# Holding GpSimd behind the first half of a Newton norm, in a fused cosine attention and MLP kernel

## Chip, cores and metric

One core of one Trainium2 chip. The metric is the device time of one execution in microseconds (us). A time is about 1.8 us longer than the span from the first to the last instruction that the same execution's profile gives.

## The reference, cut to what matters

```python
q_n = q / (np.linalg.norm(q, axis=-1, keepdims=True) + 1e-06)      # batch 8, 12 heads, 448 x 64
k_n = k / (np.linalg.norm(k, axis=-1, keepdims=True) + 1e-06)
scores = np.matmul(q_n, k_n.transpose(0, 1, 3, 2)) / tau
... softmax, @ v ...
h = x @ w_in                                  # 3584 x 768 @ 768 x 2048
g = h * (1.0 / (1.0 + np.exp(-1.702 * h)))
return (g @ w_out).astype(np.float32)
```

## The kernel before

A planner in Python simulates the engines, orders all operations and emits them in that order. GpSimd (POOL) scales q and k by their inverse norms, squares some of the q and casts v; VectorE (DVE) computes the norms. The planner takes the two to share a port of SBUF and treats it as one slot ("port") that a GpSimd operation or a norm takes. In the emitted program the slot is made real in one direction only: a GpSimd port user waits, by a semaphore wait that the planner adds (the "made wait" below), for the last VectorE port user before it in the order. "Heads" below are pairs of heads, numbered 0 to 47. Of the VectorE lines named later, L568 is the gate of the MLP's activation, and L497 and L445 normalise attention outputs.

```python
# Plan.emit
insts = emit()
insts = insts if isinstance(insts, tuple) else (insts,)
...
if ("port", 1) in takes:
    if eng == "DVE":
        port = insts[-1]
    elif port is not None:
        link(insts[0], port)          # a semaphore wait of GpSimd on VectorE
```

A norm of a group of one to three heads is planned in two operations, `norm_a` and `norm_b`. Each gives the port back at its end, so GpSimd operations may be planned between them.

```python
def norm_a(grp):
    ...
    nc.vector.tensor_scalar(out=y.bitcast(I32), in0=a.bitcast(I32), scalar1=-0.5, scalar2=RS_MAGIC, ...)   # L282
    nrms[grp] = a, y, t
    newton(grp, RS_A, RS_B)                    # returns nothing: port becomes None

def newton(grp, ca, cb):
    a, y, t = nrms[grp]
    nc.vector.scalar_tensor_tensor(out=t, in0=y, scalar=-ca, in1=y, ...)      # L295
    nc.vector.tensor_tensor(out=t, in0=t, in1=a, op=ALU.mult)                 # L298
    nc.vector.scalar_tensor_tensor(out=y, in0=t, scalar=cb, in1=y, ...)       # L299

def norm_b(grp):                               # a second newton, then 3 more
    ...
    last = nc.vector.tensor_tensor(out=y, in0=y, in1=t, op=ALU.mult)          # L310
    ...
    return last
```

## Time and profile before

| | before |
|---|---|
| median of the first 3 runs (lowest, highest) | 434.37 us (433.66, 434.76) |
| time of the profiled execution, its span | 436.03 us, 434.2 us |
| busy: TensorE, VectorE, ScalarE, GpSimd | 420.0, 242.1, 290.3, 175.1 us |
| TensorE's idle time in the span | 14.2 us |

TensorE (PE) is busy nearly throughout, so the lines to read are those of what it waited for; they are in the prediction.

### The profile page before, as it was taken

What the parts mean: (1) busy time and instruction counts of PE and PEld (TensorE: products, weight loads), DVE (VectorE), ACT (ScalarE), POOL (GpSimd) and SP (SyncE); (2) the same over time, 40 slices, a digit from 0 to 9 for tenths busy, and PEclk for the clock granted to TensorE, in tenths of its full rate; (3) what the DMA queues carried; (4) which work ended last, traced back from release to release, by engine and by line L of the source; (5) the groups of instructions that cost most, each with busy time, mean ns of one, the idle gap of its engine ahead of it and who ended that gap; (6) DMA issues with size and microseconds to landing.
All of it is one profiled execution on the core that took longest, in us unless ns stands there. A gap on an engine that the chain in (4) does not pass through costs nothing.

```text
span 434.2 us, 11090 instructions
## 1 busy us (share of the span) xinstructions
PE 420.0 (97%) x4438; PEld 260.7 (60%) x4438; DVE 242.1 (56%) x621; ACT 290.3 (67%) x460; POOL 175.1 (40%) x229
## 2 busy tenths in 40 slices
PE   7899999997999999999999999999999999999996
PEld 7668886653555555555556555565656556555564
DVE  5866887879885677838766555563332343123200
ACT  5989678955877778978794876767682864233321
POOL 0831995294868758373882817261100000000000
PEclk9999999999999999999999999999999999999999
DMA  8899997966999999787999576855112121211122
GB/s 215 201 206 272 240 195 223 261 127 169 182 223 190 197 244 223 171 183 176 170 190 220 125 175 143 167 107 111 49 26 70 31 61 43 56 38 36 38 72 74
DMA packets 98099, 64.03 MB, mean 147 GB/s; under 512 B 56320, under 2 KB 93056, under 8 KB 98048
## 3 DMA queue, kind: packets, MB, share of 16 engines
q1 hardware_dynamic: 92320, 57.03, 57.8%
q0 software_dynamic: 5696, 6.29, 8.8%
q8 instruction: 35, 0.57, 0.6%
q14 instruction: 16, 0.13, 0.1%
q10 hardware_dynamic: 32, 0.01, 0.0%
HBM read 45.61 MB, written 11.01 MB: 130 GB/s over the span
## 4 chain that ended last, share of the span: by engine, by line
PE 82%; DVE 7%; ACT 4%; issue 2%; POOL 2%; DMA 1%; SPq 0%; ACTq 0%; POOLq 0%
PE mm L611 34%; PE mm L534 15%; PE mm L552 11%; PE avp L431 8%; PE sp L405 7%; PE sp L467 2%; PE mm L484 2%; ACT et L416 2%; DVE n L269 2%; PE mm L581 2%; DVE gT L568 2%; DVE y L282 1%; DMA k<-in_k_dram 1%; ACT sq L263 1%; PE tps L375 1%
## 5 line engine op out<-in xcount | busy, mean ns | idle before, releaser
L416 ACT ACTIVATE et<-sp 112x896 f16<-112x896 f32 x192 | 170.0, 919 | 30.9 <-PE sp L405 25.2
L611 PE MATMUL mm<-w_out,gT 128*128 128x384 f16 (+1 forms) x912 | 158.4, 323 | 0.0
L611 PEld LDWEIGHTS <-gT 128*128 128x128 f16 x912 | 83.9, 98 | 60.6 <-issue 11.0
L568 DVE SCALAR_TENSOR_TENSOR gT<-th,mm 128x448 f16<-128x448 f16 x112 | 66.8, 615 | 64.2 <-ACT th L563 64.2
L563 ACT ACTIVATE th<-mm 128x448 f16<-128x448 f32 x128 | 67.6, 549 | 42.8 <-PE mm L534 36.3
L534 PE MATMUL mm<-xT,w_in 128*128 128x448 f16 x408 | 85.3, 353 | 3.2 <-DVE gT L568 3.0
L269 DVE TENSOR_REDUCE n<-sq 112x8 f32<-112x512 f32 x96 | 63.8, 679 | 22.2 <-ACT sq L263 12.9
L623 ACT ACTIVATE ost<-mm 128x384 f32<-128x384 f32 (+1 forms) x57 | 27.7, 487 | 62.2 <-PE mm L611 61.8
L534 PEld LDWEIGHTS <-w_in 128*128 128x128 f16 x408 | 37.7, 98 | 39.8 <-issue 8.9
L359 POOL CAST vt<-v 112x256 f16<-112x256 f32 x90 | 34.0, 402 | 58.6 <-PE avp L431 52.3
L552 PE MATMUL mm<-xT,w_in 64*128 64x448 f16 x528 | 57.1, 349 | 0.0
L343 POOL TENSOR_TENSOR qks<-k,y 112x512 f16<-112x512 f32 x38 | 39.6, 1042 | 34.6 <-DVE y L310 17.9
L431 PEld LDWEIGHTS <-et 112*128 112x128 f16 x1152 | 43.4, 97 | 14.7 <-issue 4.2
L431 PE MATMUL avp<-vt,et 112*128 112x65 f16 x1152 | 47.0, 193 | 0.5 <-DVE xf L445 0.4
L442 DVE RECIPROCAL rcx<-avp 128x4 f32<-128x4 f32 x72 | 12.9, 179 | 60.9 <-PE avp L431 60.9
L262 POOL TENSOR_TENSOR sq<-q 112x512 f32<-112x512 f32 x33 | 34.1, 1039 | 24.4 <-ACT et L416 9.0
L405 PE MATMUL sp<-qkT 64*128 64x448 f16 x288 | 43.3, 353 | 0.0
L343 POOL TENSOR_TENSOR qks<-q,y 112x512 f16<-112x512 f32 x38 | 39.6, 1042 | 0.0
L552 PEld LDWEIGHTS <-w_in 64*128 64x128 f16 x528 | 25.6, 94 | 20.9
L263 ACT ACTIVATE sq<-k 112x512 f32<-112x512 f32 x48 | 30.3, 635 | 3.0 <-DMA k<-in_k_dram 3.0
L445 DVE TENSOR_TENSOR xf<-avp,rcx 128x256 f16<-128x256 f32 x72 | 30.5, 424 | 2.5
L405 PEld LDWEIGHTS <-qkT 64*128 64x128 f16 x288 | 13.4, 94 | 14.6 <-issue 6.3
(48 smaller groups left out, 282.9 us busy)
## 6 DMA issues: line engine op xcount, KB each, us to landing
k<-in_k_dram SPq DMA_DIRECT2D x48, 224.0 KB, 4.6
q<-in_q_dram SPq DMA_DIRECT2D x48, 224.0 KB, 4.7
v<-in_v_dram SPq DMA_DIRECT2D x48, 224.0 KB, 4.2
w_in<-in_moe_w_in_dram POOLq DMA_DIRECT2D x2, 1536.0 KB, 15.5
w_out<-in_moe_w_out_dram POOLq DMA_DIRECT2D x2, 1536.0 KB, 15.7
out_dram<-ost SPq DMA_DIRECT2D x7, 336.0 KB, 4.7
out_dram<-ost SPq DMA_DIRECT2D x8, 288.0 KB, 3.2
out_dram<-ost SPq DMA_DIRECT2D x8, 240.0 KB, 3.1
```

Source lines behind the costliest of these rows:

```text
L262: return nc.gpsimd.tensor_tensor(out=sqs[x, ti], in0=src, in1=src, op=ALU.mult)
L263: return nc.scalar.activation(out=sqs[x, ti], in_=src, func=AF.Square)
L269: nc.vector.tensor_reduce(out=n2s[grp][:, x - grp[0], ti], in_=sqs.pop((x, ti)), axis=AX.X, op=ALU.add,)
L343: return eng.tensor_tensor(out=qkss[x][:, 1 - ti].rearrange("p c j d -> p j c d"), in0=src, in1=rss[x][:, ti, :, :, None].to_broadcast((P, ...
L405: nc.tensor.matmul(out=sp[:, j, :S], lhsT=keys(x, j, c), rhs=queries(x, j, 0, S), start=True, stop=True,)
L416: nc.scalar.activation(out=e[:, : 2 * S].rearrange("p (j s) -> p j s", j=2), in_=sps.pop(key)[:P, :, :S], func=AF.Exp, scale=inv_tau, **kw,)
L431: nc.tensor.matmul(out=ps[:, (D + 1) * t : (D + 1) * (t + 1)], lhsT=exps[x, c][:, q0 : q0 + 128], rhs=values(x, c, D * j, D * j + D + 1), ...
L534: nc.tensor.matmul(out=ps[:, :S], lhsT=w_in_sb[:, kk, 128 * m : 128 * (m + 1)], rhs=xTs[b, kk][:, :S], start=(kk == 0), stop=(kk == KT1 - 1),)
L552: insts.append(nc.tensor.matmul(out=mms[b, m + i][:, :S], lhsT=w_in_sb[rows, kk, 128 * (m + i) : 128 * (m + i + 1)], rhs=xTs[b, kk][rows, :S],
L563: nc.scalar.activation(out=ths[key], in_=mms[key][:, :S], func=AF.Tanh, scale=0.851)
L568: nc.vector.scalar_tensor_tensor(out=gT[:, m, (b % 2) * S : (b % 2 + 1) * S], in0=ths.pop((b, m)), scalar=1.0, in1=mms.pop((b, m))[:, :S], ...
L611: nc.tensor.matmul(out=mms[b2, t, n][:, : c1 - c0], lhsT=gT[:, kk, 128 * t : 128 * (t + 1)], rhs=w_out_sb[:, kk, c0:c1], start=(kk == 0), ...
```

## The change

Its intent: the first half of a norm shall hold back GpSimd's next port users by the same made wait that every other VectorE port user causes. `norm_a` now returns its last instruction (L299), so `port` holds it in place of `None`.

```diff
-        newton(grp, RS_A, RS_B)
+        return newton(grp, RS_A, RS_B)
 
     def newton(grp, ca, cb):
...
-        nc.vector.scalar_tensor_tensor(
+        return nc.vector.scalar_tensor_tensor(
             out=y, in0=t, scalar=cb, in1=y, op0=ALU.add, op1=ALU.mult
         )
```

Nothing else moves: the instructions of every engine stand in the same order in both programs.

## The prediction

> **What bounds the kernel now.** I read the page first: the busy shares, the row of TensorE in the forty slices, and the chain that ended last.
>
> ```profile
> PE 420.0 (97%) x4438; PEld 260.7 (60%) x4438; DVE 242.1 (56%) x621; ACT 290.3 (67%) x460; POOL 175.1 (40%) x229
> ...
> PE   7899999997999999999999999999999999999996
> ...
> PE 82%; DVE 7%; ACT 4%; issue 2%; POOL 2%; DMA 1%; SPq 0%; ACTq 0%; POOLq 0%
> ```
>
> TensorE is the bound almost everywhere, so only what removes an idle stretch of TensorE can shorten the span. The row shows two slices that are not full away from both ends' ramps: the tenth digit is a 7, that is 97.7 to 108.6 us (a slice is 434.2 / 40 = 10.86 us). Next I asked for TensorE's waits between 60 and 130 us (what it waited for, total us, times, longest):
>
> ```profile
> PE mm L534 <- DVE gT L568: 3.0, 2, 2.9
> PE mm L507 <- DVE xs L497: 0.9, 1, 0.9
> PE avp L431 <- DVE xf L445: 0.4, 2, 0.3
> ```
>
> All three point at VectorE, which is in order: something in its queue ahead of the gate (L568) and of the normalisation (L497) was late. The same view from 130 us to the end lists nothing, and TensorE is busy 50.00 of 50 us in each of the stretches 200 to 250, 300 to 350 and 350 to 400. The timeline from 96.5 to 103.2 us (start, duration) names the culprit:
>
> ```profile
> 96.51 0.74 POOL L359 CAST vt<-v 112x256 f16<-112x256 f32 x2
> ...
> 97.21 1.04 POOL L262 TENSOR_TENSOR sq<-q 112x512 f32<-112x512 f32 x1
> 97.26 4.11 DVE L282 TENSOR_SCALAR y<-n 112x48 int32<-112x48 int32 x1
> ...
> 98.20 2.13 POOL L359 CAST vt<-v 112x256 f16<-112x256 f32 x6
> ...
> 100.28 1.04 POOL L262 TENSOR_TENSOR sq<-q 112x512 f32<-112x512 f32 x1
> ...
> 102.01 1.14 DVE L568 SCALAR_TENSOR_TENSOR gT<-th,mm 128x448 f16<-128x448 f16 x2
> ...
> 102.68 0.73 PE L534 MATMUL mm<-xT,w_in 128*128 128x448 f16 x3 [2.86 <-DVE gT L568]
> ```
>
> L282, the first instruction of a norm, has a median of 189 ns over its 13 executions; here it takes 4110 and ends at 101.37, just after GpSimd's run of square, six casts and square ends at 101.32. The gates behind it come 4 us late, no PSUM bank is freed, and TensorE stands still for 2.86 us. The chain that ended last says the same in its steps at 97.34 (4.04 us of L282) and then 102.68 (TensorE).
>
> **What the Trainium skill says.** "SBUF — State Buffer", section "SBUF: two separate sides": the port pair that VectorE and GpSimd share is an exclusive lock held for the whole instruction, and the loser is blocked fully. The 4.11 us agree. "VectorE: DVE Perf Modes", section "The perf-mode tier table": a tensor_scalar from SBUF in a 4-byte type gets the 2x mode and tensor_tensor does not; with the section on the 2x_2P mode that makes L282 a user of both read ports. The trace agrees in that L282 is the one hit hardest. "Perfetto Trace Analysis", section "GPSIMD Engine Instruction": GpSimd's spans should be timed by their start-to-start spacing. Here that is 1.00 us for a square or scale (recorded 1.04), and I use it.
>
> **The change part by part.** It adds no arithmetic. The first half of a norm used to return nothing, and the planner stores what a VectorE port user returns as "the last port user"; with nothing stored, GpSimd operations planned after it got no wait at all until the second half was emitted. Now they wait for the first half's last instruction (L299). So it touches only GpSimd operations planned between the two halves of one norm. I walked the planner's order of the kernel before: 13 norms of this kind, of which 6 have such operations, 15 in all. In the other seven (those that begin with heads 12, 21, 27, 36, 39, 42 and 45) no GpSimd user lies between the halves and nothing changes. So the 0.82 of L282 at 128.61 stays: what it met was a scale planned before it. The six:
>
> - Heads 15 to 17 (97 us): square of 18, casts 15 to 17, square of 19. The square of 18 is held; the cast before it ends at 97.25, so L282 at 97.26 finds the port free. Four instructions at 0.19 + 0.21 + 0.21 + 0.21 and three gaps of 0.03 end the half at about 98.15 instead of 102.09: VectorE gains 3.9 us. TensorE's stalled matmul needs the first of the two gates, whose tanh is done at 97.28 + 0.54 = 97.82; the gate now ends near 98.7, before TensorE asks at 99.82. **TensorE gains 2.86 us**, all of the gap.
> - Heads 10 and 11 (66 us): scale of q 9 and cast 10. Its four instructions run from 65.89 to 68.28, 0.71 + 0.98 + 0.30 + 0.30. The first waits for an earlier scale that stays (to 66.6); the other three then take about 0.65, ending at 67.26 instead of 68.28. The normalisation (L497) moves from 68.83 to 67.8 and TensorE's 0.89 gap goes. But the scale of q 9, held from 66.52 to 67.35, ends at 68.4, and the transposes of head 9 would now start at 68.12 and need it half way: 0.2 is given back. **TensorE gains 0.7 us.**
> - Heads 18 to 20 (114 us): the half takes 0.70 + 0.33 + 0.31 + 0.97 and gaps = 2.4 us; alone 0.9. VectorE gains 1.5 us. TensorE's waits near it are 0.26 and 0.18 for L445, so **about 0.3 us**.
> - Heads 24, 30, 33: L282 ran in 0.19 in all three (143.65, 178.55, 201.57), no stall to win. The held operations are casts of values needed tens of us later and one square. **Zero.**
>
> GpSimd pays: the square of 18 moves from 97.21 to 98.25, the run ends at 102.35 instead of 101.32; the square of 21 moves by about 1.2, a cast pair by 0.5 to 3. GpSimd then idled anyway, 5.72 us before 107.04 and 3.17 before 122.34, both for the second half of the norm (L310), which VectorE now reaches about 3 us earlier. So its delay is hidden. VectorE's reduction of the square of 18 stands behind the second gate, whose tanh ends at 99.26; the square ends at 99.25. No new wait.
>
> Sum on TensorE: 2.86 + 0.7 + 0.3 = 3.9 us. What of it lasts? Its input is far ahead: head 15's transposes are issued at 109.11, land about 3.5 us later (the median), and its scores start at 123.11; later heads have more. TensorE's clock is full in every slice. I keep 0.8 of it, 3.2 us: 434.4 - 3.2 = **431.2 us**.
>
> **The rivals.**
> 1. The stall at 97.26 is a matter of 50 ns: had VectorE come that much earlier it would have had the port first. In runs without the profiler it may do so. For: 0.05 us between the two starts. Against: one norm later (114.42) loses as well, and the three runs agree within 1.1 us, while 3 us would show. If true, the gain is about 1 us: 433.4.
> 2. The made wait takes the place of the lock: GpSimd held for a late VectorE delays scales, transposes and reductions, and TensorE waits for these. For: VectorE is busy 4.90 of 5 us from 97 to 102, so holding on it is risky; casts wait in order behind the held square. Against: GpSimd idles right after each of these runs, and head 15 has 10 us to spare. If true: 434 to 436.
> 3. The gain is given back: DMA is at 9 tenths from 108 to 174 us, and TensorE 3 us earlier could meet a transfer or the activation engine. For: that row of DMA. Against: no TensorE wait on a DMA is in the list, and loads start when scales free their buffers, which come earlier too. If true, half remains: 432.5.
> 4. All of the 3.9 us lasts, and VectorE, further ahead, removes some of the other gaps of 0.15 to 0.2 us too: 430.2.
>
> **Range and chances.** The main theory (3.2 us) and rival 4 together 0.65, rival 3 0.15, rival 1 0.12, rival 2 0.08. The middle stays at 431.2; eight times in ten I expect 429.9 to 433.5. Two per cent would be 8.7 us, more than twice all the TensorE waits found, so faster by over 2% gets 0.02; slower by over 2% needs a new wait of 9 us, which nothing in the trace offers: 0.02; within 2%: 0.96.
>
> **What would show it right or wrong.** Right: L282 has no execution over 1 us; TensorE's 2.9 us wait for L568 near 100 us is gone; the tenth digit of its row is 9; VectorE's busy time falls by 5 to 7 us (4110 - 190 ns, 1.5 and 1.0 us, all from the first half); GpSimd's first square after the norm at 97 starts just after L299 ends. Wrong: TensorE shows a new wait on a GpSimd scale (L343) or a DMA transpose, or on L269's followers because reductions wait for held squares; or TensorE's idle time is as long as before with other names beside it. If the gap goes and the span stays, rival 3 holds.

## The result

| | before | after |
|---|---|---|
| median of 6 runs (lowest, highest) | 434.15 us (433.39, 435.02) | 431.94 us (431.67, 433.22) |
| ratio, 95% interval | | 0.9956 (0.9936 to 0.9976) |
| span of the profiled execution | 434.2 us | 430.0 us |
| TensorE busy, idle | 420.0, 14.2 us | 419.9, 10.1 us |
| VectorE busy | 242.1 us | 236.5 us |

A ratio is the mean time of one kernel's fast runs over that of the other's of the same rounds, so it is not quite the ratio of the medians. The interval excludes 1, though the gain is under 2%. The change is a gain of 2.2 us by the medians, inside the predicted range, but the two profiled spans differ by 4.2 us. That gap is the main question of the experiments.

The page of the kernel after (busy times, TensorE's row of forty slices, the chain that ended last):

```profile
PE 419.9 (98%) x4438; PEld 261.2 (61%) x4438; DVE 236.5 (55%) x621; ACT 290.5 (68%) x460; POOL 175.4 (41%) x229
...
PE   7889999999999999999999999999999999999996
...
PE 86%; ACT 4%; DVE 3%; issue 2%; POOL 2%; DMA 1%; SPq 0%; ACTq 0%; POOLq 0%
```

The tenth digit is 9 now, and VectorE's share of the chain fell from 7% to 3%. Of TensorE's three waits between 60 and 130 us one is left, of 0.2 us in place of 3.0:

```profile
PE mm L534 <- DVE gT L568: 0.2, 1, 0.2
```

The timeline of the kernel after at the stretch that was at 97 us (start, duration; the bracket is idle time before the instruction and what ended it):

```profile
96.03 0.75 POOL L359 CAST vt<-v 112x256 f16<-112x256 f32 x2
...
96.78 0.18 DVE L282 TENSOR_SCALAR y<-n 112x48 int32<-112x48 int32 x1
...
96.92 3.56 PE L534 MATMUL mm<-xT,w_in 128*128 128x448 f16 x18 [0.15 <-DVE gT L568]
...
97.48 0.21 DVE L299 SCALAR_TENSOR_TENSOR y<-t,y 112x48 f32<-112x48 f32 x1
97.61 0.61 DVE L568 SCALAR_TENSOR_TENSOR gT<-th,mm 128x448 f16<-128x448 f16 x1
97.83 1.04 POOL L262 TENSOR_TENSOR sq<-q 112x512 f32<-112x512 f32 x1 [1.04 <-issue]
```

L282 finds the port free and takes 0.18 us; the square is held for 1.04 us (the view names no releaser, "issue", but the wait on L299 is what the edit added) and starts 0.14 us after L299 ends at 97.69; TensorE runs 18 matmuls in one piece.

The other stretch with a visible TensorE gap, at 66 us, before:

```profile
66.52 1.04 POOL L343 TENSOR_TENSOR qks<-q,yv 112x512 f16<-112x512 f32 x1
66.64 0.98 DVE L295 SCALAR_TENSOR_TENSOR t<-y 112x32 f32<-112x32 f32 x1
...
68.89 0.27 PE L507 MATMUL mm<-ident,xs 112*128 112x112 f16 x2 [0.89 <-DVE xs L497]
69.00 0.56 PE L367 MATMUL tps<-ident,qks 112*128 112x112 f16 x8
```

and after:

```profile
66.91 0.19 DVE L295 SCALAR_TENSOR_TENSOR t<-y 112x32 f32<-112x32 f32 x1
...
67.63 1.04 POOL L343 TENSOR_TENSOR qks<-q,yv 112x512 f16<-112x512 f32 x1 [0.79 <-DVE y L299]
...
68.21 0.27 PE L507 MATMUL mm<-ident,xs 112*128 112x112 f16 x2
68.31 0.79 PE L367 MATMUL tps<-ident,qks 112*128 112x112 f16 x8
```

TensorE's gap of 0.89 is gone, and the transposes of head 9 take 0.79 in place of 0.56, because half of them wait for the scale that was held.

**A ruler that leaves the start out.** Executions differ by up to 1.9 us before 66 us, where nothing of the change acts yet. So I measure from the start of the first L282 (heads 10 and 11) to that of the sixth (heads 24 on), both from the timeline. Before:

```profile
65.89 0.71 DVE L282 TENSOR_SCALAR y<-n 112x32 int32<-112x32 int32 x1
...
143.65 0.19 DVE L282 TENSOR_SCALAR y<-n 112x48 int32<-112x48 int32 x1
```

and after:

```profile
66.17 0.71 DVE L282 TENSOR_SCALAR y<-n 112x32 int32<-112x32 int32 x1
...
139.39 0.19 DVE L282 TENSOR_SCALAR y<-n 112x48 int32<-112x48 int32 x1
```

That is 143.65 - 65.89 = 77.76 us before and 139.39 - 66.17 = 73.22 after. From the sixth to the end it is 434.2 - 143.65 = 290.55 and 430.0 - 139.39 = 290.61 us. The whole difference arises between 66 and 144 us, and nothing of it is given back later.

### The profile page after: what moved, and what is told of

It is laid out like the page before. It is cut to its first block, busy times and chain, and to the rows that moved or that the text cites. A ratio compares the mean times of both kernels' runs of the same rounds, so it can differ in the third digit from the quotient of the medians.

```text
span 430.0 us, 11091 instructions
## 1 busy us (share of the span) xinstructions
PE 419.9 (98%) x4438; PEld 261.2 (61%) x4438; DVE 236.5 (55%) x621; ACT 290.5 (68%) x460; POOL 175.4 (41%) x229
## 4 chain that ended last, share of the span: by engine, by line
PE 86%; ACT 4%; DVE 3%; issue 2%; POOL 2%; DMA 1%; SPq 0%; ACTq 0%; POOLq 0%
PE mm L611 34%; PE mm L534 17%; PE mm L552 11%; PE avp L431 8%; PE sp L405 7%; PE sp L467 2%; PE mm L484 2%; ACT et L416 2%; PE mm L581 2%; DMA k<-in_k_dram 1%; ACT sq L263 1%; DVE n L269 1%; POOL qks L343 1%; PE tps L375 1%; POOL n L326 1%
## 5 line engine op out<-in xcount | busy, mean ns | idle before, releaser
L445 DVE TENSOR_TENSOR xf<-avp,rcx 128x256 f16<-128x256 f32 x72 | 30.6, 425 | 2.5
```

## The experiments

The first four ran on one chip beside the same 11 runs of the kernel before.

### e1: the kernel before again (no edit)

> The kernel before, a second time against itself. The changed kernel's profiled span was 4.2 us shorter than that of before, but its median time only 2.2 us shorter. Theory A (the stall of L282 near 97 us, 4.1 us in the first trace, happens in every run): ratio 1.000 and a profiled span of about 434, L282 over 4 us again. Rival (a matter of 50 ns: VectorE sometimes comes first): the new trace has an L282 near 97 us well under 4 us or the run spans fall in two groups some 2 us apart.

Measured: 433.70 us, ratio to itself 1.0012 (0.997 to 1.0054), profiled span 431.5 at full clock. Its timeline:

```profile
97.32 1.04 POOL L262 TENSOR_TENSOR sq<-q 112x512 f32<-112x512 f32 x1
97.37 1.04 DVE L282 TENSOR_SCALAR y<-n 112x48 int32<-112x48 int32 x1
...
97.51 3.82 PE L534 MATMUL mm<-xT,w_in 128*128 128x448 f16 x18 [0.15 <-DVE gT L568]
98.31 2.13 POOL L359 CAST vt<-v 112x256 f16<-112x256 f32 x6
98.44 0.32 DVE L295 SCALAR_TENSOR_TENSOR t<-y 112x48 f32<-112x48 f32 x1
```

and its TensorE waits between 60 and 130 us:

```profile
PE mm L507 <- DVE xs L497: 0.9, 1, 0.9
PE avp L431 <- DVE xf L445: 0.5, 2, 0.3
PE mm L534 <- DVE gT L568: 0.2, 1, 0.2
```

VectorE again comes some 50 ns after the square, but slips in when the square ends, after 1.04 us instead of 4.11, and the 2.9 us wait of TensorE is not there. The same program has two outcomes. The ruler gives 141.01 - 66.01 = 75.00 us: the long stall costs 77.76 - 75.00 = 2.76. Theory A falls. The rival's sign came, but not its reason: VectorE did not come first, it came 46 ns after the square (43 in the first trace) and got the port one operation later.

Two lines of its page matter later: the tenth digit of TensorE's row is 9 here too, and VectorE is busy 239.4 us, though nothing was changed.

The spans also show a second lottery, that of the clock: executions at a granted clock of 0.995 or 0.996 span 433.1 in most cases (after: 431.3 to 431.8), those at 0.998 and over about 431.7 (after: 430.0). It falls in both kernels, so below I compare spans at 0.998 and over.

### e2: only the norm of heads 15 to 17 holds

```diff
-        return newton(grp, RS_A, RS_B)
+        last = newton(grp, RS_A, RS_B)
+        return last if grp[0] == 15 else None
```

> Only the norm of heads 15 to 17 hands on its last instruction; the other five stretches stay without the wait. Theory A: this alone takes the 2.9 us TensorE gap near 100 us away, so in the profile TensorE's waits fall by about 2.9 and the span by about 2.9 us against before; timed 2 to 3 us faster (ratio near 0.994). Rival (the gain lies in several stretches alike): about 1 us.

Measured: 432.92 us, ratio 0.9979 (0.9949 to 1.0009); the profiled execution was at a clock of 0.995 (span 432.8), the four at full clock span 430.9 to 431.2. L282 takes 0.18 us at this norm, as theory A expects, but the ruler gives 142.32 - 67.62 = 74.70 us, 0.30 less than e1. Where no long stall falls, this hold is worth 0.3 us and not 2.9: less than theory A (2 to 3 us timed) and than its rival (about 1 us) had it.

### e3: all but that norm hold

```diff
+        return last if grp[0] != 15 else None
```

> All stretches but that of heads 15 to 17 get the wait. Theory A: TensorE's 2.9 us gap near 100 us stays, L282 there again 3 to 4 us unless the shift of 0.5 us at 68 us changes who comes first; span about 1 us shorter than before (0.5 at 68 us, 0.5 at 118 and 124 us). Rival: most of the gain of the full change is here too (over 2 us).

Measured: 432.32 us, ratio 0.998 (0.9939 to 1.002). The profiled execution had the long stall, and TensorE's gap of 2.86 us with it:

```profile
96.25 1.04 POOL L262 TENSOR_TENSOR sq<-q 112x512 f32<-112x512 f32 x1
96.30 4.11 DVE L282 TENSOR_SCALAR y<-n 112x48 int32<-112x48 int32 x1
...
101.72 0.53 PE L535 MATMUL mm<-xT,w_in 128*128 128x448 f16 x1 [2.86 <-DVE gT L569]
```

Its clock also dipped near 100 us, so its span of 434.0 mixes two causes. The four executions at full clock span 430.0 to 430.6, within 0.6 us of the full change. The long stall needs that this one norm is not held, and removing it is what this hold does for the worst executions; in the others most of the gain is elsewhere. Up to the third L282 the trace is free of that stall: 96.30 - 65.69 = 30.61 us, as after (96.78 - 66.17 = 30.61), against 31.36 in e1. That is 0.75 us from the hold of heads 10 and 11 alone.

### e4: the changed kernel again

> The changed kernel again, on the chip of the other three. Theory A: span 430.0 at full clock, ratio to before about 0.995, equal to the product of the two partial kernels' gains within 1 us.

Measured: 431.73 us, ratio 0.9947 (0.9915 to 0.9979), span 430.1, ruler 139.56 - 66.34 = 73.22, the same as in the first trace. The ratio is within 0.5 us of the product of e2's and e3's (0.9959), as expected. The terms of the typical execution now follow on the ruler: e1 to after is 75.00 - 73.22 = 1.78 us; 0.75 of it from heads 10 and 11, 0.30 from heads 15 to 17 (e2), and the rest, 0.73, from heads 18 to 20. TensorE's timeline confirms the last term. In e1:

```profile
113.85 1.31 PE L534 MATMUL mm<-xT,w_in 128*128 128x448 f16 x6
115.42 0.64 PE L431 MATMUL avp<-vt,et 112*128 112x65 f16 x16 [0.27 <-DVE xf L445]
```

and after:

```profile
113.00 1.31 PE L534 MATMUL mm<-xT,w_in 128*128 128x448 f16 x6
114.14 0.65 PE L431 MATMUL avp<-vt,et 112*128 112x65 f16 x16
```

From the start of the first group to that of the second it is 1.57 us in e1 and 1.14 after, a gain of 0.43 where the list of waits shows 0.27: without the wait the second group starts 0.17 before the recorded end of the first. The other wait for L445 (120.97 to 121.98 in e1, 119.69 to 120.36 after) gives 0.34 in the same way.

### e5: only the norms of heads 24, 30 and 33 hold

```diff
+        return last if grp[0] in (24, 30, 33) else None
```

> Only the norms that begin with heads 24, 30 and 33 hand on their last instruction. The prediction gave these three nothing: ratio 1.000 within 0.002, TensorE's waits as before. It is also six more runs with the race at 97 us left open: theory B (L282 either slips in when the square ends, about 1.0 us, or stands to the end of the whole GpSimd run, 4.1 us) expects the spans at full clock to be 431.5, now and then 434.2, and nothing between.

Measured: 434.02 us, ratio 1.0005 (0.9969 to 1.004), ruler 142.38 - 67.37 = 75.01, L282 near 98 us 1.05 us. These three holds are worth nothing, as predicted. Of "nothing between" the spans say less: at full clock 431.9, 431.9, 432.0, 432.5, and two of the kernel before of the same rounds at 432.6 and 432.9. A late start could explain these (the traces of e2 and e5 reach the first L282 at 67.4 to 67.6 us, others at about 66), but that is not shown: those two traces ran at a clock of 0.995 and 0.996, and no execution at 432.5 to 432.9 has a trace.

### e6 and e7: one or four needless squares more in each held stretch

```diff
+            if names[i][0] == "norm":
+                held = eng == "DVE" and names[i][1] == 0
+            extra = dummy() if held and eng == "POOL" and ("port", 1) in takes else None
             insts = emit()
+            if extra is not None:
+                held = False
+                link(extra, port)      # dummy(): 1 or 4 GpSimd tensor_tensor of 112x512 on spare tiles
```

> The changed kernel with one needless square of 1.0 us on GpSimd in each of the six held stretches, held by the same wait, ahead of the held operations. Theory (GpSimd has slack after each held run): 0 to 0.7 us slower than the changed kernel. Rival (the made wait has brought GpSimd to the edge of the critical path): 2 us or more slower, with TensorE waits behind L269 or L343.

> The same with four needless squares in each stretch, 4.0 us. GpSimd's idle time after the run at 97 us is 1.6 us in the changed kernel, so 4 us no longer fit there: theory 2 to 6 us slower than the changed kernel, the waits on VectorE's reduction of the square of head 18. If it is not slower at all, GpSimd's delay does not matter and rival 2 was never near.

Measured, one square: 434.24 us; at full clock 431.1, 431.6 and 431.8, some 1.5 us over the changed kernel, more than the 0.7 of the theory and less than the 2 of the rival. The waits of TensorE between 60 and 130 us say where half of it went:

```profile
PE tps L374 <- POOL qks L350: 0.7, 1, 0.7
```

From 60 us to the end TensorE's waits sum to 1.8 us, against 0.3 in the changed kernel, so they make up the whole 1.5.

Measured, four squares: 456.03 us, ratio to before 1.0494 (1.0448 to 1.0539), profiled span 454.7, so over 24 us slower than the changed kernel where the theory had 2 to 6. TensorE's waits between 60 and 434 us are

```profile
PE avp L438 <- DVE xf L452: 4.8, 4, 2.0
PE tps L374 <- POOL qks L350: 4.0, 1, 4.0
PE mm L618 <- DVE gT L575: 2.8, 2, 2.3
PE mm L559 <- DVE gT L575: 2.8, 2, 2.6
PE mm L541 <- DVE gT L575: 2.3, 2, 2.2
```

16.7 us together; another 7.4 us is TensorE's longer busy time at a granted clock of 0.981 (427.3 against 419.9). So "GpSimd idles after each run, its delay is hidden" was too easy. Idle time right after a run does not free the work that waits for the run: the transposes of head 9 wait for the held scale, and VectorE, which is in order, stands with its gates and normalisations behind reductions of held squares (it waits 22.5 us for squares after 60 us, against 8.2 in the changed kernel). The test is not pure: the added squares take the port as well, and VectorE's own busy time grew by 0.9 us with one and by 5.4 with four, so part of the loss can be the port and not the delay. The change itself delays GpSimd by about 1 us at 66 and 97 us and gets away with 0.2 us; a microsecond more would not have.

### e8 to e11: the port race by itself

These kernels give zeros on purpose. GpSimd runs the operations of the stall, released by a VectorE copy; VectorE then copies some columns out of PSUM, more each time, and issues an instruction like L282. So its arrival moves over GpSimd's run in steps of 1 to 2 ns (some 6 in two shorter series of e8). e8 has one such copy, the others the loop below.

```diff
+    for w in [400] * more + [w]:
+        nc.vector.tensor_copy(out=wait[:, :w], in_=mm[:P, :w])
+    nc.vector.tensor_scalar(out=y.bitcast(I32), in0=n.bitcast(I32), scalar1=-0.5, scalar2=RS_MAGIC, ...)
```

> Wrong on purpose (it gives zeros): a GpSimd run of square, six casts and square released by a VectorE copy, then a VectorE copy out of PSUM of 8 to 398 elements, then an instruction like L282, 196 times with the copy longer by two elements each time; then runs of four squares and of eight casts. Theory B: the wait of the instruction depends on where in a GpSimd operation it comes: mostly it ends with the operation it meets (under 1.1 us), but in a narrow window some 40 to 50 ns after a GpSimd start it stands until the end of the run (3 to 4 us). Rival (the long stall comes from something else of that moment, as a missing semaphore): no instruction over 1.1 us.

> Wrong on purpose (zeros). The first sweep found no long stall at any moment inside the first operation of a run, so a window of 40 to 50 ns after a start is refuted. In all three traces that met the run at 97 us, L282 came not inside an operation but at the seam between two back-to-back ones: 2 ns after the recorded end of a cast in the two long stalls, 3 ns after it in the short one. This sweep moves the instruction in steps of about 1 ns over the seam from the first cast to a square (200 times) and from the first square to a cast (160 times). Theory C (the seam): one or a few steps within about 10 ns of the recorded end stand until the whole run is over, 3 to 4.5 us; all others end 43 ns after the operation they meet. Rival: none over 1.1 us, and the long stall stays unexplained.

> Wrong on purpose (zeros). The sweep before missed its aim: the instruction came 170 to 360 ns after the seam, never at it. This one is aimed with its offsets: over the seam from a first cast to a square in steps of 1 ns (twice), from a first square to a cast, and from a second cast to a square as at 97 us. Theory C (the seam): some steps within about 10 ns of the recorded end of the first operation stand until the whole run is over, 3 to 4.5 us; the others end 43 ns after the operation they meet. Rival: none over 1.2 us although the steps cover the seam, and the long stall stays unexplained.

> Wrong on purpose (zeros). In the two sweeps before, the casts wrote one buffer and waited for one another: they began 463 ns apart, with gaps of some 60 ns, while at 97 us they come 347 ns apart and overlap in the record. This run is the true one: square, two scales, two casts, then the square, six casts and square, each with its own buffer and with the casts' strided output, and the L282-like instruction moved over the seam from the second cast to the square in steps of about 1 ns (270 steps, twice). Theory D (without gaps between GpSimd operations VectorE can be passed over): some steps, at the seam or within the square, stand to the end of the run, 3 to 4.2 us. Rival: none over 1.2 us, and why L282 is passed over in some executions stays open.

e9 missed its aim (it came 170 to 360 ns after the seam); e10 met it (longest wait 1.09 us). e11 has the true run: its casts begin 347 ns apart or less, like those of the kernel. The view of the one line over all steps of e8 and of e11 (duration ns, minimum, median, maximum):

```profile
L73 DVE TENSOR_SCALAR y<-n x328: 175/815/1066, 3.1 to 1538.8; 112x48 int32<-112x48 int32 x164
```

```profile
L83 DVE TENSOR_SCALAR y<-n x540: 175/962/1101, 6.9 to 4349.2; 112x48 int32<-112x48 int32 x180
```

No step of any sweep waited for more than one whole operation. In e8 all 146 steps that came 17 ns or more after the start of the first square ended 42 to 45 ns after its recorded end. That is the short outcome. The long one, in which L282 is passed over at seven seams between GpSimd operations, did not come once in 1,710 instructions, at any of the offsets tried and with or without gaps between the operations. Theory B's window, theory C and theory D are refuted for the port alone. What decides between the two outcomes in the kernel stays open: in the two traces with the long one VectorE came 43 and 44 ns after the square's start, in the three with the short one (e12 below included) 41, 46 and 53 ns, so this offset alone does not decide it. What else the kernel had under way at that moment (other engines, DMA) is not in the sweeps and was not tested.

### e12: the kernel before, a third time

> The kernel before once more against itself, for how often the long stall falls. So far at full clock (0.998 and over) 1 of 20 executions with a recorded span shows 434.2, the others 430.8 to 432.9. If the long stall is a rare outcome of the same program (rival 1 of the prediction): most spans at full clock again near 431.6, at most a few at 434, and the trace has L282 near 97 us at 1.0 us. If it falls in a third or more of the executions, several spans at full clock near 434.

Measured: 433.47 us, ratio to itself 0.9997, span 431.7, L282 at 97.53 us 1.03 us. Over all sets that record a span the kernel before has 34 executions at a clock of 0.998 or over. One spans 434.2, the first profile; the other 33 lie between 430.8 and 432.9. The mean of all is 431.7, that of the nine of the changed kernel 430.0 (429.7 to 430.3). Of five traces in which the norm of heads 15 to 17 is not held, two have the long stall (the first profile and e3) and three the short one (e1, e5, e12). So it is rare at full clock, and I cannot say why traces caught it more often. The count leaves out slower clocks, where it may hide: of eleven executions of the kernel before at 0.995 or 0.996 nine span 432.8 to 433.3 and two 434.8 and 435.3, and e3's two at 0.995 span 434.0 (the trace with the long stall) and 434.4. The two have no trace of their own.

## Why the prediction was right or wrong

- **Mechanism: right.** The port was the cause, only stretches with GpSimd work between the halves mattered, L282 has no execution over 1 us any more (largest 0.82), and the square starts after L299. Two other signs came by luck of the first trace: the tenth digit is 9 and VectorE's busy time fell by 5.6 us (predicted 5 to 7), but e1, unchanged, has the 9 as well, and against its 239.4 us the fall is 2.9.
- **Readings that were too quick.** "The 4.11 us agree" with a lock held for a whole instruction: a square is one instruction of 1.04 us, which is e1's stall; 4.11 is a run of eight. That L282 is "the one hit hardest" holds for the long stall only: in e1 it takes 1.04, and L295 at 66.75 and L299 at 113.22 take 0.98 and 0.97. The text speaks of two slices that are not full, and the row has one. And 0.8 of 3.9 is 3.1, not 3.2.
- **Heads 15 to 17, 2.86 us: the term that was mis-sized.** It is right for the execution in the first profile, and only there: on the ruler 2.76 for the long stall and 0.30 for the rest. In a typical execution only the 0.30 is to be had. The prediction had this outcome as rival 1, at 0.12 (for another reason, that VectorE comes first, and with a gain of 1 us where 1.78 came), and put it aside with "the three runs agree within 1.1 us, while 3 us would show". That was the wrong comparison: three runs without the stall agree as well. The profiled execution's own time, 436.03 us against a median of 434.37, stood there to say that the trace was the odd one. The sum then took a gain that belongs to the long outcome off a median that belongs to the short one.
- **Heads 10 and 11, 0.7 us:** measured 0.75, the give-back at head 9's transposes included.
- **Heads 18 to 20, 0.3 us:** measured 0.73, as the rest on the ruler. The two waits of the list were the right ones, but I took 0.3 for their 0.26 + 0.18, and each was worth some 0.16 more than it is listed at (e4: 0.43 and 0.34).
- **Heads 24, 30, 33, zero:** right (e5).
- **GpSimd's delay is hidden:** true within 0.2 us for the delay that the change makes, but not for the reason given; with one more microsecond 1.5 us are lost (e6), so there is next to no slack. Rival 2 did not come, but e6's 434.24 is where it had put the time.
- **0.8 of it lasts:** all of it lasts (290.55 against 290.61 us from the sixth norm to the end). Rival 3 did not come.

So that 431.2 came so near the measured 431.94 is in part luck, with errors that offset one another: one term about 2.6 us too large, one 0.4 too small, a discount of 0.7 that was not due. The typical gain at full clock is 1.78 us on the ruler and 1.7 by the mean spans; that the medians differ by 2.2 fits with clock dips in some of those runs, but the clock of the runs of before in that set is not recorded.

## What to carry to other kernels

Before pricing a stall from one trace, compare the time of the profiled execution with the timed runs; if it is over all of them, look at a second trace first, because a race can fall either way. Where two engines share a port and one of them issues in long runs, a made wait on the short user can take the bad outcome away at little cost (here 0.2 us), provided that what the held engine feeds has time to spare, which only an added delay shows. A planner that stores a helper's return value as "the last user" drops the wait silently when the helper returns nothing.

## What the Trainium skill lacked or had wrong

- "SBUF — State Buffer", section "SBUF: two separate sides", says that the shared pair is held for a whole instruction and that the loser is blocked fully. The sweeps agree, and add the size: a VectorE instruction that meets a GpSimd square ends 42 to 45 ns after the square's recorded end (146 of 146 steps).
- The same section doesn't say who gets the pair next when GpSimd's operations follow one another. Mostly VectorE does, at the next seam; but twice in five traces L282 stood through a square, six casts and a square, 4.11 us. No page has this, and the sweeps (1,710 instructions, longest 1.10 us) did not reproduce it.
- No page has what such a held GpSimd operation costs in itself: in all six holds of the kernel after it starts 0.08 to 0.14 us after the end of the VectorE instruction that it waits for (67.63 after 67.55, 97.83 after 97.69).
